# Bucketed attention with a gated MoE: key penalties on ScalarE, and a key of its own for each piece of the first batch

## The chip, the cores and the metric

The kernel runs on one core of a Trainium2 chip. The metric is the device time of one execution in microseconds, the median of several runs. The core has five engines that run on their own and wait for one another through semaphores: TensorE (PE in the profile, PEld its weight loads), VectorE (DVE), ScalarE (ACT), GpSimd (POOL), and SyncE (SP), which issues the DMAs.

## The reference

Attention over 4 batches, 8 heads, 768 positions and 64 dimensions, in which a query sees only the keys of its own hash bucket, and then a product of two linear layers, multiplied by a third:

```
q_bits = (q @ proj) > 0          # 6 bits; the same for k
mask   = bucket(q) == bucket(k)  # 64 buckets
scores = where(mask, (q @ k.T) / 8, -1e9)
attn   = softmax(scores); attn /= sum(attn) + 1e-9
x      = (attn @ v), heads side by side  # 3072 x 512
out    = ((x @ w_a) * (x @ w_b)) @ w_out # 512 -> 1536 -> 512
```

All inputs and the output are float32.

## The kernel before

**Units of work.** A batch has four head pairs and three chunks of 256 positions; a unit is one chunk for two head pairs (a `half`), and holds 8 tiles (`qtile`): one head, 128 queries, all 768 keys. So there are 24 units and 192 tiles. After the two units of a chunk, its rows of x are complete (`su_end`: divide, transpose, split into two fp16 parts `xT`), and one MoE block (`moe`) follows for the chunk, in 12 steps f of 128 hidden columns each: 24 matmuls for the two products, a multiplication, and 6 matmuls with w_out.

**Keys and queries.** `kprep` makes for a head pair the transposed keys (`trk`) in two parts, a rounded one and the remainder, then the hash bits, then for each of the 64 buckets the number of differing bits. The contraction of the score matmul has 128 rows: 64 for the head dimension, and 64 bucket rows. In the key's bucket rows stands a penalty: 0 where the bucket is the key's own and -2^60 where it isn't, made by VectorE (line 607) from the counts in PSUM. In the query's bucket rows stands a one-hot vector, made by ScalarE's Relu (line 708). So a score of another bucket gets -2^60 within the same matmul. `qprep` does a query half. In batch 0 both use one PSUM buffer (tag "o"), later a pair of them (tag "s") that the scores use too.

**A tile.** Scores into PSUM (4 matmuls, line 734); their negated maximum on VectorE (746); bias and exponential on ScalarE (753, 761); a cast to fp16 (line 775 on VectorE, or line 770 on ScalarE for tiles whose key is under `ACT_CASTS`, which is 0); the remainder on GpSimd (780); a transposing DMA (786); 18 matmuls with the two parts of v (795).

**Weights.** w_a and w_b come in 6 groups of 4 tiles of 128x512, w_out in 12 pieces (`wo_piece`). Each tile is loaded through one of 8 staging buffers (the first four pieces of w_out have their own place), converted by two ScalarE operations (347, 355) and one VectorE operation (362) that rebuild the number in another layout, and then split: w_a and w_b into two fp16 parts after a maximum over the group (392, 412, 417), w_out into two parts (428, 431). MoE step f needs the two groups of its third of the hidden columns, and its piece of w_out. All of that happens once, beside the first batch.

**The order.** Every operation is entered into a plan with its engine, an assumed duration, the buffers that it needs and a key, which is a priority and not a time: `Plan.issue` walks through an assumed time and, whenever an engine is free, gives it the operation with the lowest key among those that are ready and whose buffers can be had. What comes out is a fixed order for each engine (the DMAs in SP's too). Tile u of the unit that starts at `start` has the key `start + u`; a unit is 8 keys long. Preparations have keys some steps earlier (`K_LEAD`, `Q_LEAD`, `V_LEAD`), MoE blocks some later (`M_LAG`), the weight groups `W_FIRST + W_PACE * g`. `DVE_BESIDE` and `POOL_BESIDE` are what the plan adds where VectorE and GpSimd work on SBUF at the same time.

The key pairs of the first batch had the keys -7, -6.5, 1 and 3, its query halves -9, -1, 7, 15, 23 and 31, its v pairs -2, -1, 6 and 7; the weight groups 8, 10, 12, 14, 16 and 18, the pieces of w_out 20 (f 0 to 3), 24 and 28; the MoE blocks of the first two chunks 24 and 40, with 1.33 for each step.

Of the kernel before, what the change touches and what calls it, by code (L numbers as in the profile page):

```python
# [20 lines left out]
P = 128  # L21
# [10 lines left out]
NCH = S // CH  # L32
TPC = CH // P

NE, NA, NAT, NO = 3, 2, 2, 2
ACT_CASTS = 0
W_FIRST, W_PACE, WO_LAG = 8.0, 2.0, 8.0
M_LAG = 8.0  # L40
K_LEAD, Q_LEAD, V_LEAD = 7, 9, 2
S_LAG = -1.0
BIG = float(2.0**60)
ESC = float(2.0**14)
LN_ESC = float(14.0 * np.log(2.0))
# [3 lines left out]
def constants():  # L49

    c = np.zeros((P, P + 2), np.float32)
    c[:, :P] = np.eye(P)
    sets = (np.arange(NBUCK)[:, None] >> np.arange(NBITS)) & 1
    c[:, P] = 1 - np.tile(sets.sum(1), 2)
    c[:, P + 1] = -np.tile(sets.sum(1), 2)
    w = np.zeros((P, 2, P), np.float16)
    for j in range(2):
        for h in range(2):  # L60
            row = (2 * j + h) * NBITS
            col = NBUCK * (1 - h)
            w[row : row + NBITS, j, col : col + NBUCK] = 1 - 2 * sets.T
    return c, w
# [8 lines left out]
T_ISSUE = 1.4  # L73


DVE_BESIDE, POOL_BESIDE = 0.3, 0.15


class Buf:
# [140 lines left out]
def attention_moe(ctx: ExitStack, tc: tile.TileContext, q, k, v, proj, w_a, w_b, w_out, cst, cst_w, out):  # L220
# [19 lines left out]
    def flat2(ap):  # L240
        return ap.rearrange("p (a b) -> p a b", a=2)
# [181 lines left out]
    def wo_piece(f, key):  # L423

        y = buf("osb", [P, DM], F32, f"wo_y{f}", NO)
        after = [("words", f)] if f >= NF - NSTG else []
        to_f32(w_out[f * P : (f + 1) * P], f, f"wo{f}", key, lambda: y.t, [y], after)
        op("ACT", 0.6, lambda: nc.scalar.copy(out=wo[f].t[:, :DM], in_=y.t), key, r=[y], w=[(wo[f], 0)])
        op(
            "DVE", 0.7,  # L430
            lambda: nc.vector.tensor_tensor(
                out=wo[f].t[:, DM:], in0=y.t, in1=f32(wo[f].t[:, :DM]), op=ALU.subtract
            ),
            key, r=[y, (wo[f], 0)], w=[(wo[f], 1)], sbuf=True,
        )
# [75 lines left out]
    def kprep(b, hp, key, tag):  # L511

        n = f"{b}_{hp}"
        tr = [buf("trk", [P, 2, S], F32R, f"trk_{n}_{h}", NH) for h in range(2)]
        trk[b, hp] = tr
        raw = buf("raw", [P, NT, 2, D], F32, f"rk_{n}")
        for h in range(2):
            op(  # L520
                "SP", DMA_ISSUE,
                lambda h=h: nc.sync.dma_start(
                    out=raw.t[:, :, h, :], in_=k[b, 2 * hp + h].rearrange("(p t) d -> p t d", t=NT)
                ),
                key - 1, w=[(raw, h)], svc=1.1,
            )
        ps = psum(f"pk_{n}", tag)

        def tps():
            for t in range(NT):  # L530
                nc.tensor.transpose(  # L531
                    out=ps.t[:, t // 3, (t % 3) * P : (t % 3 + 1) * P],
                    in_=raw.t[:, t].rearrange("p h d -> p (h d)"), identity=ident,
                )

        op("PE", 0.7, tps, key, r=[(raw, 0), (raw, 1), "csb"], w=[ps], hold=tr)
        for h in range(2):
            op(
                "ACT", 0.81,
                lambda h=h: nc.scalar.activation(  # L540
                    flat2(tr[h].t[own[h], 0]), ps.t[own[h], :, :HALF], AF.Copy, scale=SCALE
                ),
                key, r=[ps], w=[(tr[h], "hi")],
            )
            op(
                "ACT", 0.81,
                lambda h=h: nc.scalar.activation(  # L547
                    flat2(tr[h].t[own[h], 1]), ps.t[own[h], :, :HALF], AF.Copy, scale=SCALE
                ),
                key, r=[ps], w=[(tr[h], "hi2")],  # L550
            )
            op(
                "DVE", 0.96,
                lambda h=h: nc.vector.scalar_tensor_tensor(  # L554
                    out=flat2(tr[h].t[oth[h], 1]), in0=ps.t[own[h], :, :HALF], scalar=SCALE,
                    in1=flat2(f32(tr[h].t[own[h], 0])), op0=ALU.mult, op1=ALU.subtract,
                ),
                key, r=[ps, (tr[h], "hi")], w=[(tr[h], "lo")],
            )
        exact = b == 0  # L560
        psb = psum(f"kb_{n}", tag)

        def rows():
            for j in range(2):
                cols = slice(j * HALF, (j + 1) * HALF)
                bit_rows(psb.t[:, j, :HALF], [(h, tr[h].t[:, 1, cols]) for h in range(2)], exact)

        op(
            "PE", 1.5 if exact else 0.75, rows, key,
            r=["pjw"] + [(tr[h], x) for h in range(2) for x in ("hi2", "lo")], w=[psb],  # L570
        )
        if exact:
            op(
                "DVE", 0.94,
                lambda: nc.vector.tensor_scalar(
                    out=flat2(bits_k[:NROW]), in0=halves(psb.t, NROW), scalar1=0.0, scalar2=None,
                    op0=ALU.is_gt,
                ),
                key, r=[psb], w=["bits_k"],
            )  # L580
        else:
            neg = buf("e", [P, S], F32, f"neg_{n}", NE)
            op(
                "ACT", 0.8, lambda: nc.scalar.mul(flat2(neg.t[:NROW]), psb.t[LOB:MB, :, :HALF], -1.0),
                key, r=[psb], w=[neg],
            )
            op(
                "DVE", 0.96,
                lambda: nc.vector.tensor_tensor(
                    out=flat2(bits_k[:NROW]), in0=halves(psb.t, NROW), in1=flat2(neg.t[:NROW]), op=ALU.is_gt  # L590
                ),
                key, r=[psb, neg], w=["bits_k"],
            )
        pso = psum(f"ko_{n}", tag)

        def diffs():
            for j in range(2):
                nc.tensor.matmul(
                    pso.t[:, j, :HALF], lhsT=wbit[:, 0, :], rhs=bits_k[:, j * HALF : (j + 1) * HALF],
                    start=True, stop=True,  # L600
                )

        op("PE", 0.35, diffs, key, r=["bits_k", "wbit"], w=[pso])
        for h in range(2):
            op(
                "DVE", 1.02,
                lambda h=h: nc.vector.tensor_scalar(
                    out=flat2(tr[h].t[oth[h], 0]), in0=pso.t[oth[h], :, :HALF], scalar1=neg_n[oth[h]],
                    scalar2=-BIG, op0=ALU.is_gt, op1=ALU.mult,
                ),  # L610
                key, r=[pso, "csb"], w=[(tr[h], "pen")],
            )

    def qprep(b, c, half, key, tag):
# [90 lines left out]
        for h in range(2):  # L705
            op(
                "ACT", 0.68,
                lambda h=h: nc.scalar.activation(  # L708
                    trq[h].t[oth[h], :, 0, :], flat2(pso.t[oth[h], 0]), AF.Relu, bias=one_n[oth[h]],
                    scale=-1.0,  # L710
                ),
                key, r=[pso, "csb"], w=[(trq[h], "hot")],
            )
# [231 lines left out]
    for b in range(NB):  # L945
        base = per * 6 * b
        for i, (c, half) in enumerate((c, half) for c in range(NCH) for half in range(2)):
            start = base + per * i
            tag = "o" if start < 2 * per else "s"
            if i < 2:  # L950
                for hp in (2 * half, 2 * half + 1):
                    kprep(b, hp, start - K_LEAD + (hp % 2) * (2 if b or half else 0.5), tag)
            qprep(b, c, half, start - Q_LEAD, tag)
            if i == 0:
                v_scale(b, start - 9 if b else -3)
            if i < 2:
                for hp in (2 * half, 2 * half + 1):
                    vprep(b, hp, start - V_LEAD + hp % 2)
            st = su_state(b, c, half)
            u = 0  # L960
            for j in range(2):
                for h in range(2):
                    for t in range(TPC):
                        qtile(b, c, half, j, h, t, st, start + u)
                        u += 1
            su_end(b, c, half, st, start + per - 1, "o" if start < 2 * per else "s")
            if b == 0 and i == 1:
                for g in range(NG):
                    w_group(g, W_FIRST + W_PACE * g)
                for f in range(NF):  # L970
                    wo_piece(f, W_FIRST + W_PACE * (f // 4 * 2 + 2) + WO_LAG)
            if half == 1:
                m = b * NCH + c
                moe(b, c, 2 * per * (m + 1) + M_LAG, 2 * per / NF, m == NB * NCH - 1)
    with tc.manual_schedule():
        plan.issue()

# [32 lines left out]
```

## Time and profile before

| | |
|---|---|
| median of 3 runs | 1033.65 us (1031.47 to 1034.38) |
| the profiled execution | 1032.79 us |
| its span, from the first to the last instruction | 1030.7 us |
| TensorE, weight loads | busy 941.3 us, 794.7 us |
| VectorE, ScalarE, GpSimd | busy 656.7, 597.7, 436.3 us |
| mean granted TensorE clock | 0.96 of full speed |

The profile is of one execution. "Busy" counts the time in which an engine works on an instruction, without register, branch and semaphore instructions. A row of a group of instructions gives line, engine, operation, output and input with their shapes, the count, then the summed busy time and the mean of one in ns, then the idle time of the engine just before them and what ended it.

### The profile page before, as it was taken

How to read it: one execution, taken by the hardware profiler on the slowest of the kernel's cores; microseconds unless marked ns; L12 is line 12 of the kernel's file. 1: busy time of each engine (PE TensorE's matmuls, PEld its weight loads, DVE VectorE, ACT ScalarE, POOL GpSimd, SP SyncE). 2: the span in 40 equal slices, each digit the busy share in tenths (PEclk: the TensorE clock that was granted, in tenths of full speed). 3: DMA queues.
4: the chain of work that ended last, by engine and by line, in shares of the span. 5: the costliest groups of instructions: out<-in, count | busy, mean ns of one | idle time of the engine just before them, and what ended most of it. 6: DMA issues, size and time to landing. Idle time of an engine off the chain costs nothing.

```text
span 1030.7 us, 22648 instructions
## 1 busy us (share of the span) xinstructions
PE 941.3 (91%) x9132; PEld 794.7 (77%) x9132; DVE 656.7 (64%) x984; ACT 597.7 (58%) x1251; POOL 436.3 (42%) x340
## 2 busy tenths in 40 slices
PE   3555568999999999999999999999999999999998
PEld 1434457888888888888788888888888888888886
DVE  3998999877767556557767556566776665544111
ACT  5787775656666655546666655556766655544221
POOL 0112344545544555544344445544435445455111
PEclk9757679999999999999999999999999999999999
DMA  8787766577565656676556666766556555565000
GB/s 286 239 205 210 160 136 109 90 149 171 104 132 113 110 105 128 113 149 124 123 93 130 103 99 123 149 128 129 116 124 113 103 113 93 98 122 96 16 22 21
DMA packets 370152, 127.44 MB, mean 124 GB/s; under 512 B 353920, under 2 KB 362368, under 8 KB 370048
## 3 DMA queue, kind: packets, MB, share of 16 engines
q1 hardware_dynamic: 370048, 126.00, 59.1%
q8 instruction: 72, 1.18, 0.5%
q14 instruction: 32, 0.26, 0.1%
HBM read 44.18 MB, written 6.29 MB: 49 GB/s over the span
## 4 chain that ended last, share of the span: by engine, by line
PE 77%; DVE 13%; ACT 7%; issue 2%; SPq 0%; DMA 0%; POOLq 0%; POOL 0%; DVEq 0%; ACTq 0%
PE ab L879 33%; PE o L921 18%; PE s L734 12%; PE av L795 8%; DVE trk L554 2%; ACT trk L540 2%; ACT trk L547 2%; PE qb L505 2%; DVE mx L746 1%; DVE wab L417 1%; PE kb L505 1%; DVE wab L362 1%; PE pq L638 1%; PE pk L531 1%; DVE a L775 1%
## 5 line engine op out<-in xcount | busy, mean ns | idle before, releaser
L780 POOL TENSOR_TENSOR a<-e,a 128x768 f16<-128x768 f32 x192 | 327.4, 1706 | 386.6 <-DVE a L775 316.4
L879 PE MATMUL ab<-xT,wab 128*128 128x256 f16 x3456 | 418.4, 274 | 1.7 <-DVE g L901 1.4
L879 PEld LDWEIGHTS <-wab 128*128 128x128 f16 x3456 | 325.0, 98 | 64.9 <-issue 28.6
L746 DVE TENSOR_REDUCE mx<-s 128x1 f32<-128x768 f32 x192 | 181.9, 951 | 103.5 <-PE s L734 102.0
L921 PE MATMUL o<-wo,g 128*128 128x512 f32 x864 | 233.4, 405 | 0.3 <-ACT g L908 0.2
L734 PE MATMUL s<-trk,trq 128*128 128x384 f32 x768 | 185.3, 368 | 30.6 <-ACT e L761 27.4
L911 POOL TENSOR_TENSOR g<-g,g 128x256 fp32r<-128x256 f32 x144 | 111.6, 775 | 201.7 <-ACT g L908 190.2
L761 ACT ACTIVATE e<-s,bias 128x768 f32<-128x768 f32 x192 | 172.9, 900 | 16.8 <-POOL a L780 6.4
L921 PEld LDWEIGHTS o<-wo,g 128*128 128x128 f32 x864 | 153.9, 189 | 27.9 <-ACT g L908 0.7
L734 PEld LDWEIGHTS s<-trk,trq 128*128 128x128 f32 x768 | 136.2, 200 | 38.9 <-ACT e L761 30.9
L901 DVE SCALAR_TENSOR_TENSOR g<-ab,absc,a 128x256 f32<-128x256 f32 x144 | 69.3, 481 | 138.9 <-ACT a L893 111.8
L753 ACT ACTIVATE bias<-mx,lnc 128x1 f32<-128x1 f32 x192 | 56.2, 293 | 171.4 <-DVE mx L746 170.7
L795 PEld LDWEIGHTS <-at 128*128 128x128 f16 x3456 | 124.0, 100 | 26.3 <-issue 21.2
L795 PE MATMUL av<-vh,at 128*128 128x64 f16 x2304 | 133.7, 196 | 1.4 <-DMA at<-a 1.2
L775 DVE CAST a<-e 128x768 f16<-128x768 f32 x192 | 117.9, 616 | 16.5 <-ACT e L761 9.8
L893 ACT ACTIVATE a<-ab,absc 128x256 f32<-128x256 f32 x144 | 68.2, 474 | 95.6 <-PE ab L879 94.0
L908 ACT CAST g<-g 128x256 fp32r<-128x256 f32 x144 | 58.0, 403 | 43.4 <-DVE g L901 41.4
L795 PE MATMUL av<-vl,at 128*128 128x64 f16 x1152 | 66.6, 195 | 1.7 <-DVE vl L491 1.7
L554 DVE SCALAR_TENSOR_TENSOR trk<-pk,trk 64x768 fp32r<-64x768 f32 x32 | 30.6, 955 | 29.8 <-ACT trk L547 20.7
L658 DVE TENSOR_TENSOR trq<-pq,trq 64x512 fp32r<-64x512 f32 x48 | 32.9, 686 | 19.1 <-ACT trq L653 16.9
L708 ACT ACTIVATE trq<-qo,csb 64x512 fp32r<-64x512 f32 x48 | 32.8, 683 | 15.2 <-PE qo L699 14.7
L648 ACT CAST trq<-pq 64x512 fp32r<-64x512 f32 x48 | 27.7, 578 | 21.2 <-PE pq L638 11.2
(77 smaller groups left out, 676.9 us busy)
## 6 DMA issues: line engine op xcount, KB each, us to landing
rq<-in_q_dram SPq DMA_DIRECT2D x96, 64.0 KB, 2.3
rk<-in_k_dram SPq DMA_DIRECT2D x32, 192.0 KB, 3.5
raw_w<-in_moe_w_a_dram SPq DMA_DIRECT2D x12, 512.0 KB, 6.2
raw_w<-in_moe_w_b_dram SPq DMA_DIRECT2D x12, 512.0 KB, 5.6
raw_wo<-in_moe_w_out_dram SPq DMA_DIRECT2D x12, 512.0 KB, 4.3
vm<-in_v_dram SPq DMA_DIRECT2D x16, 384.0 KB, 3.8
vr<-in_v_dram SPq DMA_DIRECT2D x16, 384.0 KB, 3.4
out_dram<-osb SPq DMA_DIRECT2D x24, 256.0 KB, 2.3
```

Source lines behind the costliest of these rows:

```text
L734: nc.tensor.matmul(ps.t[:, jj, :HALF], lhsT=trq.t[:, j, i, t * P : (t + 1) * P], rhs=tr.t[:, i, jj * HALF : (jj + 1) * HALF], start=i == 0 ...
L746: lambda: nc.vector.tensor_reduce(out=mx.t[:, u : u + 1], in_=halves(ps.t), axis=AX.XY, op=ALU.max, negate=True),
L761: lambda: nc.scalar.activation(flat2(e.t), halves(ps.t), AF.Exp, bias=bias.t[:, u : u + 1], scale=1.0, accum_out=sm.t[:, u : u + 1],),
L775: "DVE", 0.55, lambda: nc.vector.tensor_copy(out=a2.t[:, 0], in_=e.t), key,
L780: lambda: nc.gpsimd.tensor_tensor(out=a2.t[:, 1], in0=e.t, in1=a2.t[:, 0], op=ALU.subtract),
L795: nc.tensor.matmul(av.t[:, u, :], lhsT=at.t[:, a + kt, :], rhs=w.t[:, h, kt, :], start=i == 0, stop=i == 3 * NT - 1,)
L879: nc.tensor.matmul(pl.t[:, m, :CH], lhsT=wt(m, wi, cc, f), rhs=xi.t[:, cc, :], start=i == 0, stop=i == 3 * NC - 1,)
L893: lambda a=a, pl=pl, gr=gr: nc.scalar.activation(a.t, pl.t[:, 0, :CH], AF.Copy, scale=absc[:, b, gr : gr + 1]),
L901: lambda a=a, g32=g32, pl=pl, gr=gr: nc.vector.scalar_tensor_tensor(out=g32.t, in0=pl.t[:, 1, :CH], scalar=absc[:, b, gr + 1 : gr + 2], in ...
L908: op("ACT", 0.41, lambda g=g, g32=g32: nc.scalar.copy(out=g[0].t, in_=g32.t), kf - 8, r=[g32], w=[g[0], "order_g0"])
L911: lambda g=g, g32=g32: nc.gpsimd.tensor_tensor(out=g[1].t, in0=g32.t, in1=f32(g[0].t), op=ALU.subtract),
L921: nc.tensor.matmul(po.t[:, u, :], lhsT=g[gi].t[:, us], rhs=wo[f].t[:, wi * DM : (wi + 1) * DM], start=f == 0 and i == 0, stop=f == NF - 1 ...
```

## The change

- The penalties are made by ScalarE: Sign of (-count - n) with the bias n per row, which gives 0 for the own bucket and -1 for others. The factor 2^60 moves into the queries' one-hot rows: Relu with a scale of -2^60 and a bias multiplied by 2^60.
- In the first batch each key pair, query half, v pair, weight group, third of w_out and MoE block gets a key of its own.
- The casts of the first 16 tiles (keys under 16) go to ScalarE.
- In the later batches keys are prepared 10.5 steps ahead (7 before), queries 5 (9 before); MoE blocks lag by 7 (8 before).
- The plan assumes 0.5 and 0.25 us for VectorE and GpSimd beside one another (0.3 and 0.15 before).

```diff
-ACT_CASTS = 0
-W_FIRST, W_PACE, WO_LAG = 8.0, 2.0, 8.0
-M_LAG = 8.0
-K_LEAD, Q_LEAD, V_LEAD = 7, 9, 2
+ACT_CASTS = 16
+K_LEAD, Q_LEAD, V_LEAD = 10.5, 5, 2
+M_LAG = 7.0
+K0 = [-11.5, -8.5, -6.5, 6.5]
+V0 = [-2.0, -1.5, 7.0, 8.5]
+Q0 = [-5.5, 2.5, 11.0, 11.0, 29.5, 33.0]
+VS0 = -3.0
+WG0 = [11.0, 9.0, 11.5, 14.0, 19.5, 23.0]
 S_LAG = -1.0
+WO0 = [13.5, 17.0, 39.0]
+M0 = [19.0, 40.0]
+M0_PACE = [1.48, 1.33]
...
-    c[:, P] = 1 - np.tile(sets.sum(1), 2)
+    c[:, P] = BIG * (1 - np.tile(sets.sum(1), 2))
...
-DVE_BESIDE, POOL_BESIDE = 0.3, 0.15
+DVE_BESIDE, POOL_BESIDE = 0.5, 0.25
...
-                "DVE", 1.02,
-                lambda h=h: nc.vector.tensor_scalar(
-                    out=flat2(tr[h].t[oth[h], 0]), in0=pso.t[oth[h], :, :HALF], scalar1=neg_n[oth[h]],
-                    scalar2=-BIG, op0=ALU.is_gt, op1=ALU.mult,
+                "ACT", 0.81,
+                lambda h=h: nc.scalar.activation(
+                    flat2(tr[h].t[oth[h], 0]), pso.t[oth[h], :, :HALF], AF.Sign,
+                    bias=neg_n[oth[h]], scale=-1.0,
...
-                    scale=-1.0,
+                    scale=-BIG,
...
-                    kprep(b, hp, start - K_LEAD + (hp % 2) * (2 if b or half else 0.5), tag)
-            qprep(b, c, half, start - Q_LEAD, tag)
+                    kprep(b, hp, start - K_LEAD + 2 * (hp % 2) if b else K0[hp], tag)
+            qprep(b, c, half, start - Q_LEAD if b else Q0[i], tag)
...
-                v_scale(b, start - 9 if b else -3)
+                v_scale(b, start - 9 if b else VS0)
...
-                    vprep(b, hp, start - V_LEAD + hp % 2)
+                    vprep(b, hp, start - V_LEAD + hp % 2 if b else V0[hp])
...
-                    w_group(g, W_FIRST + W_PACE * g)
+                    w_group(g, WG0[g])
                 for f in range(NF):
-                    wo_piece(f, W_FIRST + W_PACE * (f // 4 * 2 + 2) + WO_LAG)
+                    wo_piece(f, WO0[f // 4])
...
-                moe(b, c, 2 * per * (m + 1) + M_LAG, 2 * per / NF, m == NB * NCH - 1)
+                first = m < len(M0)
+                moe(
+                    b, c, M0[m] if first else 2 * per * (m + 1) + M_LAG,
+                    M0_PACE[m] if first else 2 * per / NF, m == NB * NCH - 1,
+                )
```

## Rows read from the trace of the kernel before

**Rows 1.** The head of the page: span, then busy time and share of each engine.
```profile
span 1030.7 us, 22648 instructions
PE 941.3 (91%) x9132; PEld 794.7 (77%) x9132; DVE 656.7 (64%) x984; ACT 597.7 (58%) x1251; POOL 436.3 (42%) x340
```

**Rows 2.** Busy time by stage: stretch, its length, engines, clock, DMA share, GB/s.
```profile
0.00:153.00 153.00, 80.05 (x521) 59.22 (x522) 126.41 (x181) 111.74 (x202) 35.57 (x22) 0.74 0.77 206
153.00:190.00 37.00, 32.82 (x329) 27.09 (x327) 36.73 (x53) 23.39 (x49) 17.95 (x12) 0.95 0.56 101
190.00:940.00 750.00, 742.69 (x7584) 637.65 (x7582) 476.37 (x719) 441.71 (x954) 362.36 (x283) 1.00 0.62 119
940.00:1031.00 91.00, 85.76 (x707) 70.78 (x704) 17.21 (x33) 20.88 (x49) 20.41 (x24) 1.00 0.13 30
```

**Rows 3.** The same table for parts of the first 153 us.
```profile
30.00:153.00 123.00, 70.14 (x489) 54.02 (x490) 114.45 (x163) 93.46 (x173) 35.37 (x18) 0.68 0.75 183
20.00:90.00 70.00, 36.24 (x176) 25.47 (x177) 62.97 (x91) 58.03 (x103) 11.07 (x6) 0.72 0.87 251
...
20.00:153.00 133.00, 74.74 (x501) 56.15 (x502) 121.29 (x170) 102.26 (x188) 35.37 (x18) 0.70 0.77 200
```

**Rows 4.** Waits of 0 to 153 us: who for whom, total us, times, longest.
```profile
POOL a L780 <- DVE a L775: 105.5, 12, 38.5
```

**Rows 5.** Timeline of ScalarE at 152 us: start, length, instruction.
```profile
151.87 0.59 ACT L842 CAST xT<-px 128x512 f16<-128x512 f32 x1 [2.02 <-PE px L831]
```

**Rows 6.** Groups of VectorE, 0 to 153 us.
```profile
L362 DVE SCALAR_TENSOR_TENSOR wab<-raw_w 128x512 int32<-128x512 int32 x23 | 20.1, 883 | 2.2 <-ACT raw_w L355 1.9
L746 DVE TENSOR_REDUCE mx<-s 128x1 f32<-128x768 f32 x21 | 19.8, 948 | 1.2 <-PE s L734 1.0
L417 DVE SCALAR_TENSOR_TENSOR wab<-wab,wsc 128x512 f16<-128x512 f32 x20 | 18.9, 945 | 0.0
L775 DVE CAST a<-e 128x768 f16<-128x768 f32 x18 | 12.0, 665 | 0.1
L392 DVE TENSOR_REDUCE wmx<-wab 128x1 f32<-128x2048 f32 x5 | 11.4, 2275 | 0.1
L607 DVE TENSOR_SCALAR trk<-ko,csb 64x768 fp32r<-64x768 f32 x8 | 8.1, 1016 | 0.4 <-PE ko L598 0.2
```

**Rows 7.** Groups of ScalarE, 0 to 153 us.
```profile
L761 ACT ACTIVATE e<-s,bias 128x768 f32<-128x768 f32 x20 | 18.0, 900 | 3.7 <-POOL a L780 3.0
L355 ACT ACTIVATE raw_w<-raw_w 128x512 int32<-128x512 uint8 x24 | 15.9, 661 | 0.0
...
L412 ACT ACTIVATE wab<-wab,wsc 128x512 f16<-128x512 f32 x20 | 14.3, 716 | 4.9 <-DVE wab L417 4.7 <-DVE wsc L321 0.2
L347 ACT ACTIVATE raw_wo<-raw_wo 128x512 f32<-128x512 f32 x11 | 7.4, 670 | 1.4 <-DMA raw_wo<-in_moe_w_out_dram 1.4
...
L540 ACT ACTIVATE trk<-pk 64x768 fp32r<-64x768 f32 x8 | 6.4, 805 | 11.0 <-PE pk L531 6.6 <-DVE trk L554 4.4
...
L486 ACT ACTIVATE vh<-vr,vs 128x768 f16<-128x768 f32 x4 | 3.7, 921 | 0.4 <-DVE vs L321 0.4
```

**Rows 8.** Timeline of TensorE: first query half and key pair, first scores of both halves.
```profile
6.09 1.44 PE L638 MATMUL pq<-csb,rq 128*128 128x128 f32 x4 [6.09 <-DMA rq<-in_q_dram]
...
15.96 1.54 PE L531 MATMUL pk<-csb,rk 128*128 128x128 f32 x6 [1.47 <-ACT trq L708]
...
29.72 1.65 PE L734 MATMUL s<-trk,trq 128*128 128x384 f32 x4 [0.26 <-DVE trk L607]
...
88.03 2.88 PE L734 MATMUL s<-trk,trq 128*128 128x384 f32 x8 [1.92 <-DVE trk L607]
```

**Rows 9.** Groups of TensorE, 300 to 940 us.
```profile
L734 PE MATMUL s<-trk,trq 128*128 128x384 f32 x556 | 127.0, 352 | 0.8 <-ACT e L761 0.7
```

**Rows 10.** One line by itself, 0 to 190 us: shortest, median, longest in ns.
```profile
L417 DVE SCALAR_TENSOR_TENSOR wab<-wab,wsc x23: 729/737/2126, 47.0 to 182.2; 128x512 f16<-128x512 f32 x23
```

**Rows 11.** Groups of ScalarE over the whole span: the only table load.
```profile
L648 ACT ACT_TABLE_LOAD x1 | 1.3, 1283 | 0.7 <-PEq L989 0.7
```

## The prediction

> **What bounds the kernel now.** I read four views, in this order. The head of the page first: TensorE is busy 91% of 1030.7 us, VectorE 64%, ScalarE 58%, so in the mean TensorE is the bound [rows 1]. Then the table by stage, which shows that this mean mixes two regimes [rows 2]. From 190 to 940 us TensorE is busy 742.69 of 750 us at full clock, and nothing that relieves another engine can be worth more there than the 7.3 us that are left. From 0 to 153 us it is busy 80.05 us at a mean granted clock of 0.74: 73 us idle. Between lies a short ramp (37 us, 4.2 idle), and the last 91 us have 5.2 idle. The third view says who fills the first 153 us: VectorE, busy 114.45 of the 123 us between 30 and 153 (93%); ScalarE is at 76% there, and at 83% in its dense stretch from 20 to 90 us [rows 3]. The waits of this stretch agree: GpSimd stood 105.5 us for the fp16 cast on VectorE [rows 4]. The fourth view is the event that ends the regime. The chunk of x that the first MoE block needs is cast at 151.87 us [rows 5], and its matmuls start there. So the bound of the start is the work of VectorE, with ScalarE close behind, up to that event; the rest is TensorE's own work.
>
> What can't have been needed by then is in the same place: at 153 us VectorE has unpacked 23 of the 24 weight tiles and split 20 of them, and has reduced 21 score tiles, where the first chunk needs 16 [rows 6]. The weights went ahead of the attention.
>
> **The change, part by part.**
>
> *Penalties to ScalarE.* Each key pair has two, 1016 ns on VectorE, 8 in the first batch [rows 6]: 8 x 1.016 = 8.1 us off VectorE before the event. The trace has no Sign. The nearest row is ScalarE's copy of the same shape from PSUM, 64x768 to fp32r with a plain scale, 805 ns; the split of v, 768 columns with a scale read per partition as the bias is here, takes 921 [rows 7]. Nothing below the copy is to be had for the same columns, so 0.80 to 0.92 us; I take 0.81: 8 x 0.81 = 6.5 us onto ScalarE (at most 7.4). The 24 of the later batches move beside a full TensorE: ScalarE has 441.7 busy of 750 there [rows 2], 24 x 0.81 = 19 us take it from 59 to 61%. Cost nothing; without TensorE as cover it would be those 19 us.
>
> *One-hot rows scaled by 2^60.* Same instruction, another constant: nothing.
>
> *Casts to ScalarE.* The first 16 tiles' casts: 16 x 0.665 = 10.6 us off VectorE [rows 6]. ScalarE's row for it doesn't exist before; the ends are again the copy of 768 columns with a plain scale, 0.805, and the v split, which writes the same 128x768 fp16, 0.921 [rows 7]. The scale is plain here, so 0.82: 16 x 0.82 = 13.1 us (to 14.7). The cast now follows its exponential on the same engine instead of queueing behind weight work, which is the longest wait of [rows 4]; what is late next is ScalarE itself.
>
> *Order of the weights.* Groups 4 and 5 go from the keys 16 and 18 to 19.5 and 23, the wo pieces of f 8 to 11 from 28 to 39. Before, they already stood behind the first 16 tiles (keys 0 to 15) and were done first all the same, because the second half's scores waited for their key pair until 88.03 us [rows 8]; that pair's key goes from 1 to -6.5. By 153 us VectorE had spent on groups 4 and 5: 7 unpackings, 4 splits and one maximum, 7 x 0.883 + 4 x 0.945 + 2.275 = 12.2 us [rows 6]. ScalarE: 8 x 1.32 + 4 x 0.716 = 13.4 us, and the two conversions of 7 of the 11 wo pieces, 7 x 1.33 = 9.3 us [rows 7]. The order is by key only among what is ready, so a part is still done early, in the gap that the next paragraph shows. Between none and all of it I take two thirds, as all these keys move back and the gate of the second half's scores opens earlier: 8.1 us on VectorE, 15.1 on ScalarE. Of the tiles beyond 16 (5 reductions x 0.948, 4 exponentials x 0.900) half: 2.4 and 1.8 us [rows 6, 7].
>
> *Order of the preparation.* Three key pairs now stand ahead of the first query half. All use one PSUM buffer (tag "o"), one after the other: before, the query half took 6.09 to 15.96 us and the first pair 15.96 to its first scores at 29.72 [rows 8]. Three pairs of 14 us and the query's 10 put the first score tile at about 6 + 42 + 10 = 58 us. SP loads in the same order, with two raw buffers, and the v loads come behind them. That gap is filled by weight work (24 tiles, each with 1.8 us of VectorE, 0.883 + 0.945, and 2.0 of ScalarE, 2 x 0.661 + 0.716); what it costs if the cover fails is the second rival.
>
> *The sum.* VectorE up to the event: 126.4 - 8.1 - 10.6 - 8.1 - 2.4 = 97.2 us. ScalarE: 111.7 + 6.5 + 13.1 - 15.1 - 1.8 = 114.4 us [rows 2]. VectorE, with 11.9 us done by 30 us (126.4 - 114.45) and 93% from then on, would be there at 122 us, so ScalarE decides now. By 20 us it has done 9.5 (111.74 less the 102.26 of 20 to 153 [rows 3]); the other 104.9 at 93%, what the engine that binds reached, with its own 83% as the lower end, last 113 us: 133 us. The event comes 20 us earlier. Two score tiles fewer lie done then, 8 matmuls of 0.228 us (127.0 over 556) [rows 9] = 1.8 us that TensorE still has to do. Gain 18 us: 1032.79 - 18 = 1015 us. The profiled execution lies 0.9 us under the median of the three runs, 1033.65, so I leave it at 1015.
>
> *Later batches.* Key preparation 3.5 keys earlier, query preparation 4 later. A key is 4.6 us there (139 tiles in 640 us [rows 9]), so 5 keys of lead are 23 us for a chain of 10. Bounds: the 7.3 us idle of 190 to 940 all gone, or doubled; I take zero. MoE one key earlier leaves 4.6 us less behind the last attention tile: 0 to +4.6, I take zero. The new allowances for VectorE beside GpSimd only alter the order. What they deal with is real: a split takes 737 ns in the median and 2126 beside GpSimd [rows 10]. The mean of 945 over that median is 4.2 us on the 20 splits by 153 us; bounds 4.2 either way, on VectorE, which is not the bound of my sum.
>
> **Table loads.** The trace has one activation table load, 1283 ns at the start, and Exp, Prelu, Relu, Copy and Identity run behind it without another [rows 11]. The Trainium skill, ScalarE: Activation LUTs, section Table sets, says that functions come in named sets and that each switch of set costs about 2.7 us with its drain; its list for the set of exp gives only some of its functions, and Sign is not among those named. With Sign in the set my sum stands; without it, at the page's price, 4 pairs x 2 switches add an estimated 21 us to ScalarE. A rule of the same page, that cheap functions sit in every set, speaks for the first. The rival below goes by the row.
>
> **The rivals.**
> 1. *Larger gain.* All of the deferred weight work and all tiles beyond 16 stay behind the event: ScalarE has 111.7 + 19.6 - 22.7 - 3.6 = 105.0 us, 20 + 95.5/0.93 = 123 us, 30 us earlier, less 4 tiles or 3.6 us: 1006 us; with the key pairs ready sooner, down to 990. For it: the later keys. Against: idle engines take whatever is ready. The end of this road is 73 us.
> 2. *Slower: ScalarE becomes the bound behind a late first score.* Scores start near 58 us, and ScalarE stays at 83% with nothing deferred: 131.3 us of work, 20 + 121.8/0.83 = 167 us, 14 us later than now, with no tile fewer done: 1047 us. It decides from the point where the chunk is cast after 151 us. For it: 83% is what this engine reached [rows 3]; exponential and cast now cost it 0.90 + 0.82 = 1.7 us for each tile. Against: the bottleneck VectorE gives up 18.7 us, and the casts no longer queue.
> 3. *Gain given back in the ramp.* The chunk is ready early, but group 4 and 5 and the late wo pieces aren't: 12.2 us on VectorE and 8 wo pieces, each with an unpacking of 0.883 and a remainder of the same 512 columns, for which I take the same (14 us), fall into the 40 us after the event, where VectorE is 99% busy already (36.73 of 37) [rows 2, 6]. If half of those 26 us shows, 1015 + 13 = 1028 us.
> 4. *Sign is in another set.* 8 to 16 loads of 1.283 us on the ScalarE of the first batch, at 93%: 11 to 22 us, 1026 to 1037.
>
> **How the numbers follow.** Forecast (1007 to 1025) 0.50; rival 1 (990 to 1007) 0.24; rival 3 0.13; rival 2 0.10; rival 4 0.03. The range reaches into rival 1 to 991 and past rival 3 to 1036, and leaves out rival 2 and a tail below. About 0.3%, 3 us, is what a measurement can tell from no change. Faster than that: 0.50 + 0.24 + half of rival 3 and a third of rival 4 = 0.82; within: the middle of rival 3 and a share of rival 4, 0.07; slower: rival 2 and what is left, 0.11.
>
> **What would show it.** The cast of the first chunk near 133 us; TensorE over 90% busy within 10 us of it; ScalarE over 88% from 20 us to there and VectorE under it; Sign at 0.8 us and a single table load; first score near 58 us; 190 to 940 us unchanged. The prediction is wrong if the cast comes after 150 us, if TensorE idles more than 10 us in the 40 us behind it, or if the time moves with those marks in place.

## The result, and the profile after

The changed kernel takes 1020.29 us (median of 4 runs, 1019.93 to 1020.85) against 1033.59 for the kernel before: ratio 0.9875, 95% interval 0.9858 to 0.9892, 13.3 us less. The forecast was 1015 us, 18 less.

The head of the page, beside [rows 1]:

```profile
span 1018.4 us, 22624 instructions
PE 937.7 (92%) x9132; PEld 790.6 (78%) x9132; DVE 611.0 (60%) x936; ACT 634.8 (62%) x1299; POOL 433.0 (43%) x340
```

VectorE lost 45.7 us and ScalarE gained 37.1; TensorE is still busy for all but 81 us (89 before). Busy time by stage, beside [rows 2, 3]; the columns are those of [rows 2]:

```profile
0.00:143.00 143.00, 75.42 (x514) 53.77 (x514) 98.09 (x145) 116.01 (x203) 32.20 (x22) 0.75 0.75 199
143.00:190.00 47.00, 44.36 (x450) 37.67 (x451) 44.48 (x67) 36.86 (x77) 25.18 (x18) 0.96 0.76 163
190.00:930.00 740.00, 734.16 (x7475) 629.92 (x7474) 449.06 (x692) 460.79 (x972) 355.24 (x279) 1.00 0.62 119
...
20.00:143.00 123.00, 70.38 (x498) 51.28 (x498) 92.32 (x133) 107.13 (x191) 32.00 (x18) 0.71 0.73 187
...
930.00:1018.40 88.40, 83.73 (x697) 69.21 (x695) 19.39 (x34) 21.16 (x48) 20.37 (x23) 0.99 0.16 35
```

The two engines have changed places: from 20 us to the end of the first stage ScalarE is busy 107.13 of 123 us (87%), VectorE 75%. Two numbers carry the comparisons below. From 190 us on the granted clock is full, so TensorE's busy time from there to the end is the work that the start left undone: 734.16 + 83.73 = 817.9 us here, 742.69 + 85.76 = 828.5 before [rows 2]. The rest of the span behind 190 us is TensorE's idle time: 1018.4 - 190 - 817.9 = 10.5 us here, 12.2 before. So of the span's 12.3 us, 10.6 come from work done earlier and 1.7 from less idle time later.

Timeline of TensorE at the first scores and of ScalarE at the cast that completes the first chunk, beside [rows 5, 8]:

```profile
55.38 2.93 PE L744 MATMUL s<-trk,trq 128*128 128x384 f32 x8 [0.77 <-ACT trq L718]
...
142.72 0.59 ACT L852 CAST xT<-px 128x512 f16<-128x512 f32 x1 [0.20 <-PE px L841]
```

The first score comes at 55 us (58 forecast), the chunk at 142.7 (133 forecast, 151.87 before). The groups of ScalarE and then of VectorE from 0 to 143 us, beside [rows 7] and [rows 6]:

```profile
L357 ACT ACTIVATE raw_w<-raw_w 128x512 f32<-128x512 f32 x21 | 13.9, 664 | 0.1
...
L780 ACT CAST a<-e 128x768 f16<-128x768 f32 x16 | 13.2, 824 | 0.4 <-DMA at<-a 0.4
L422 ACT ACTIVATE wab<-wab,wsc 128x512 f16<-128x512 f32 x16 | 11.4, 711 | 0.1
L617 ACT ACTIVATE trk<-ko,csb 64x768 fp32r<-64x768 f32 x8 | 7.2, 896 | 5.7 <-PE ko L608 5.7
...
L357 ACT ACTIVATE raw_wo<-raw_wo 128x512 f32<-128x512 f32 x5 | 3.3, 660 | 0.0
...
L550 ACT ACT_TABLE_LOAD x1 | 1.3, 1283 | 0.7 <-PEq L1003 0.7
```

```profile
L756 DVE TENSOR_REDUCE mx<-s 128x1 f32<-128x768 f32 x21 | 20.0, 952 | 6.2 <-PE s L744 6.0
L427 DVE SCALAR_TENSOR_TENSOR wab<-wab,wsc 128x512 f16<-128x512 f32 x16 | 14.7, 921 | 5.6 <-ACT wab L422 5.5
L372 DVE SCALAR_TENSOR_TENSOR wab<-raw_w 128x512 int32<-128x512 int32 x19 | 13.0, 695 | 3.0 <-ACT raw_w L365 2.9
```

Sign takes 896 ns, the cast 824, and there is one table load. Of groups 4 and 5 nothing is split yet (16 splits are groups 0 to 3), and 5 pieces of w_out are begun instead of 11: the deferral took place. The score tiles are as many as before, 21 reductions.

### The profile page after: what moved, and what is told of

It reads as the page before. It is cut to its first block, busy times and chain, and to the rows that moved or that the text cites. A ratio compares the mean times of both kernels' runs of the same rounds, so it can differ in the third digit from the quotient of the medians.

```text
span 1018.4 us, 22624 instructions
## 1 busy us (share of the span) xinstructions
PE 937.7 (92%) x9132; PEld 790.6 (78%) x9132; DVE 611.0 (60%) x936; ACT 634.8 (62%) x1299; POOL 433.0 (43%) x340
## 4 chain that ended last, share of the span: by engine, by line
PE 76%; ACT 5%; DVE 3%; issue 1%; DMA 0%; POOL 0%; POOLq 0%; DVEq 0%; ACTq 0%
PE ab L889 34%; PE o L931 18%; PE s L744 11%; PE av L805 8%; DVE trk L564 1%; ACT trk L550 1%; ACT trk L557 1%; PE qb L515 1%; PE px L841 1%; PE pq L648 1%; ACT e L771 1%; PE kb L515 1%; ACT trk L617 1%; PE qo L709 0%; DMA at<-a 0%
## 5 line engine op out<-in xcount | busy, mean ns | idle before, releaser
L790 POOL TENSOR_TENSOR a<-e,a 128x768 f16<-128x768 f32 x192 | 323.4, 1684 | 374.0 <-DVE a L785 214.6
L805 PEld LDWEIGHTS <-at 128*128 128x128 f16 x3456 | 121.9, 99 | 33.2 <-issue 22.1
L785 DVE CAST a<-e 128x768 f16<-128x768 f32 x176 | 105.9, 602 | 40.9 <-ACT e L771 34.3
L718 ACT ACTIVATE trq<-qo,csb 64x512 fp32r<-64x512 f32 x48 | 32.8, 684 | 15.9 <-PE qo L709 15.4
L550 ACT ACTIVATE trk<-pk 64x768 fp32r<-64x768 f32 x32 | 25.7, 805 | 24.6 <-DVE trk L564 13.8
```

The source lines that it names most:

```text
L785: "DVE", 0.55, lambda: nc.vector.tensor_copy(out=a2.t[:, 0], in_=e.t), key,
L790: lambda: nc.gpsimd.tensor_tensor(out=a2.t[:, 1], in0=e.t, in1=a2.t[:, 0], op=ALU.subtract),
L805: nc.tensor.matmul(av.t[:, u, :], lhsT=at.t[:, a + kt, :], rhs=w.t[:, h, kt, :], start=i == 0, stop=i == 3 * NT - 1,)
```

## The experiments

Twelve kernels. "Keys" are the first batch's. "Left" is TensorE's busy time from 190 us to the end, "idle" the rest of the span behind 190 us, both of the one profiled execution; the median and the ratio to the kernel before (95% interval) are of all runs. Each kernel was timed beside fresh runs of the kernel before, whose median was 1033.1 us for Sign, Sign + casts, - Sign - casts and - casts, 1032.3 for Sign in batches 1 to 3, - Sign, - keys and - later leads, and 1032.4 for the last four; the ratios go by these.

| kernel | median us | ratio | chunk cast at | left | idle |
|---|---|---|---|---|---|
| before | 1033.6 | | 151.9 | 828.5 | 12.2 |
| the change | 1020.29 | 0.9875 [0.9858, 0.9892] | 142.7 | 817.9 | 10.5 |
| before + Sign | 1028.69 | 0.9960 [0.9947, 0.9973] | 155.1 | 827.4 | 9.1 |
| before + Sign in batches 1 to 3 | 1029.25 | 0.9968 [0.9956, 0.9979] | 151.2 | 828.1 | 9.8 |
| before + Sign + casts | 1029.52 | 0.9966 [0.9953, 0.9979] | 159.1 | 829.9 | 8.7 |
| change - Sign - casts | 1037.45 | 1.0037 [1.0023, 1.0052] | 151.4 | 827.5 | 19.3 |
| change - casts | 1030.26 | 0.9978 [0.9969, 0.9988] | 152.6 | 826.6 | 13.9 |
| change - Sign | 1034.41 | 1.0019 [1.0010, 1.0029] | 153.0 | 826.8 | 15.9 |
| change - keys | 1032.22 | 0.9995 [0.9985, 1.0004] | 158.2 | 832.0 | 8.5 |
| change - later leads | 1023.77 | 0.9910 [0.9895, 0.9925] | 145.2 | 820.5 | 12.4 |
| change, allowance 0.45 | 1028.03 | 0.9959 [0.9946, 0.9973] | 147.5 | 823.3 | 15.1 |
| change, old allowances | 1026.26 | 0.9936 [0.9922, 0.9951] | 144.4 | 821.0 | 14.5 |
| change, 8 casts | 1026.29 | 0.9937 [0.9922, 0.9951] | 149.6 | 823.3 | 11.7 |
| change, two PSUM tags | 1029.15 | 0.9960 [0.9947, 0.9974] | 147.8 | 825.1 | 13.0 |

**Sign alone, on the old keys.** The three hunks of the penalty and the one-hot rows, and nothing else:

```diff
-                "DVE", 1.02,
-                lambda h=h: nc.vector.tensor_scalar(
...
+                "ACT", 0.81,
+                lambda h=h: nc.scalar.activation(
+                    flat2(tr[h].t[oth[h], 0]), pso.t[oth[h], :, :HALF], AF.Sign,
...
-                    scale=-1.0,
+                    scale=-BIG,
```

> The kernel before with one part of the change: penalties by Sign on ScalarE and 2^60 in the one-hot rows; keys, casts and allowances as before. Load theory (the start lasts as long as the engine with the most work up to the first chunk of x): VectorE loses 8 x 1.016 us, at 93% the chunk comes 8.7 us earlier, 1025 us (1022 to 1028). Order theory (the start lasts as long as the attention's own chain, which the keys set; loads have slack): 1030 to 1035.

1028.69 us lies between the two, and neither is how it came about. The chunk came 3 us later, and the work left at 190 us is 1 us less; the gain is idle time behind 190 us, 12.2 to 9.1. That asked for the next one.

**Sign in the later batches alone.**

```diff
-                "DVE", 1.02,
+                "ACT" if b else "DVE", 0.81 if b else 1.02,
```

(with VectorE's form for b = 0, times -1.)

> The kernel before with Sign on ScalarE in the batches 1 to 3 alone; the first batch's 8 penalties stay on VectorE (times -1 instead of -2^60, the factor in the one-hot rows). Keys as before. The run with Sign everywhere gained 4.4 us, although its first chunk came 3 us later. Later-batch theory: those 24 penalties shorten the key chain in batches 1 to 3, TensorE's idle time of 190 to 930 us falls from 7.3 to about 4.5, and the whole is 1030 to 1031. First-batch theory: the gain comes from the start, this one stays at 1032 to 1034 with 7 us idle in 190 to 930.

1029.25: the later-batch theory, and a little more. The start is that of the kernel before (from 0 to 143 us TensorE is busy 74.57 us, 73.26 before; the chunk comes within 0.7 us of it). The waits of TensorE for the key remainder and its twin, between 190 and 930 us (who for whom, total us, times, longest), before and then in this kernel:

```profile
PE kb L505 <- DVE trk L554: 4.3, 5, 1.4
PE qb L505 <- DVE trq L658: 1.4, 2, 0.7
```

```profile
PE kb L505 <- DVE trk L554: 1.5, 2, 0.9
PE kb L505 <- ACT trk L547: 1.2, 1, 1.2
...
PE qb L505 <- DVE trq L661: 0.7, 1, 0.7
```

Here kb and qb are the hash bits of keys and queries. Before, it was VectorE that kept a key pair's bits waiting even where TensorE is 99% busy. With 24 penalties fewer TensorE waits there 1.5 us for VectorE and 1.2 for ScalarE, instead of 4.3 for VectorE.

**Sign and casts on the old keys.** As the first, with `ACT_CASTS = 16`.

> The kernel before with Sign and with the first 16 casts on ScalarE, all keys, leads and allowances as before. Load theory: VectorE loses 18.7 us, but ScalarE has 131 us of work up to the first chunk with nothing deferred, which at 93% ends at 151 us: no gain over the kernel before, 1028 to 1036. Order theory: 1028 to 1035 as well, the casts' shorter queue worth a few us at most. A third possibility, that engine placement is the whole effect: 1020.

1029.52: both theories had that range, so the time doesn't decide between them; the third possibility, 1020, is out. In the profile the chunk comes at 159.1 us, 7 later than before and 4 later than with Sign alone, so the casts bring the start nothing on the old keys.

**Keys, leads and allowances alone.** The changed kernel with `ACT_CASTS = 0` and VectorE's penalties.

> The changed kernel with the penalties back on VectorE and no casts on ScalarE: only keys, leads, lag and allowances are new. Load theory: VectorE has about 116 us up to the first chunk, which comes near 142 us, 1023 us (1019 to 1028). Order theory: the whole gain stands, 1018 to 1022. Placement is everything: 1031 to 1036.

1037.45, slower than before and above all three ranges. This order without the new division of work is no gain: the chunk stays at 151.4 us, and behind it TensorE idles 14.7 us between 190 and 930 us, twice what it did:

```profile
190.00:930.00 740.00, 725.33 (x7369) 622.26 (x7367) 461.21 (x701) 435.73 (x935) 344.73 (x273) 1.00 0.61 117
```

**The change without the casts.**

```diff
-ACT_CASTS = 16
+ACT_CASTS = 0
```

> The changed kernel with the first 16 casts back on VectorE. Load theory: ScalarE, the busiest of the changed start, loses 13.2 us and VectorE gains 10.6 us, so both stand near 105 us up to the first chunk; it comes near 135 us, 1012 us (1008 to 1017). Order theory: the casts queue behind weight work on VectorE again, and GpSimd with them; the chunk comes 5 to 10 us later, 1024 to 1030.

1030.26. The load theory, with its 1012, is out: with 13 us of casts taken from the busiest engine the chunk came 10 us later. The order theory's range ended at 1030. On these keys taking the casts off ScalarE costs 10 us, on the old ones nothing; but 6 to 9 us is what another order alone can cost (below), so the 10 are not shown to be the casts' own.

The load theory took ScalarE's other work as given, and it wasn't. The stretch up to the chunk, first in the changed kernel and then in this one, and under it this one's chunk and two groups of ScalarE from 0 to 153 us:

```profile
0.00:142.72 142.72, 75.42 (x514) 53.77 (x514) 97.81 (x144) 115.73 (x203) 31.92 (x22) 0.75 0.75 199
0.00:152.59 152.59, 78.86 (x513) 56.63 (x514) 117.55 (x181) 118.90 (x211) 36.32 (x22) 0.80 0.75 207
```

```profile
152.59 0.59 ACT L852 CAST xT<-px 128x512 f16<-128x512 f32 x1 [1.62 <-PE px L841]
L357 ACT ACTIVATE raw_w<-raw_w 128x512 f32<-128x512 f32 x24 | 15.9, 664 | 0.0
L357 ACT ACTIVATE raw_wo<-raw_wo 128x512 f32<-128x512 f32 x11 | 7.3, 666 | 0.0
```

ScalarE was busy 118.9 us up to the chunk, more than the 115.7 with the casts in it. All 24 tiles and 11 pieces of w_out were begun by then, against 21 and 5: weight work on ScalarE (conversions and splits) is 63.6 us instead of 48.0. The deferral went with the casts. Whether the weights went ahead because the attention was waiting, or the attention waited because they were ahead, these rows don't tell.

**The change without Sign.** The penalty hunks undone, casts and keys as changed.

> The changed kernel with the penalties back on VectorE; keys and casts as changed. Additive theory: Sign is worth 4 to 7 us, as between the runs without casts (1037.5 and 1030.3): 1024 to 1028. Joint theory (the keys fit only the full division of work): most of the gain is lost, 1029 to 1035. If casts and keys alone do it: 1020 to 1022.

1034.41, the joint theory: without Sign nothing is left of the gain. The chunk comes at 153.0 us, and TensorE idles 15.9 us behind 190.

**The change without its keys.**

```diff
-K0 = [-11.5, -8.5, -6.5, 6.5]
+K0 = [-7, -6.5, 1, 3]
...
-WG0 = [11.0, 9.0, 11.5, 14.0, 19.5, 23.0]
+WG0 = [8.0, 10.0, 12.0, 14.0, 16.0, 18.0]
```

(V0, Q0, WO0, M0 and its pace likewise.)

> The changed kernel with the first batch's keys of before (key pairs -7, -6.5, 1, 3 and so on); Sign, casts, later leads and allowances as changed. Additive theory: the keys cost 4 us by themselves, so this is faster than the change, 1014 to 1018. Joint theory: as Sign and casts on the old keys, 1028 to 1032, since the keys are what lets the casts on ScalarE pay.

1032.22: 0.2 us above the joint theory's range, and 14 above the additive one's. Timeline of this kernel, exponentials of ScalarE, and under it the maxima of the last two weight groups on VectorE:

```profile
61.38 0.89 ACT L771 ACTIVATE e<-s,bias 128x768 f32<-128x768 f32 x1
...
86.12 0.90 ACT L771 ACTIVATE e<-s,bias 128x768 f32<-128x768 f32 x1 [1.41 <-POOL a L790]
...
110.45 0.90 ACT L771 ACTIVATE e<-s,bias 128x768 f32<-128x768 f32 x1
```

```profile
75.32 2.29 DVE L402 TENSOR_REDUCE wmx<-wab 128x1 f32<-128x2048 f32 x1
89.15 1.75 DVE L402 TENSOR_REDUCE wmx<-wab 128x1 f32<-128x1536 f32 x1
```

The same two groups in the changed kernel:

```profile
145.29 2.27 DVE L402 TENSOR_REDUCE wmx<-wab 128x1 f32<-128x2048 f32 x1
172.21 1.74 DVE L402 TENSOR_REDUCE wmx<-wab 128x1 f32<-128x1536 f32 x1
```

On the old keys VectorE has the maxima of the last two groups, those of the last third of the hidden columns, done by 92 us, and one exponential starts between 62 and 110 us. On the new ones these groups come 70 and 83 us later, and ten exponentials start between 62 and 110 us. I take this for the lever of the change. The keys alone don't pull it: with the casts on VectorE the weights were early again and the chunk came at 152.6 us.

**The change with the old leads in the later batches** (`K_LEAD, Q_LEAD` 7 and 9, `M_LAG` 8).

> The changed kernel with K_LEAD 7, Q_LEAD 9 and M_LAG 8 of before in the later batches. My prediction put them at zero (bounds 7.3 us either way): 1018 to 1022. If the later leads cost (idle of 190 to 930 was 14.7 us with the new keys, leads and allowances alone): faster, 1015 to 1018; if they gain: 1022 to 1026.

1023.77, 3.5 us slower than the change. That is in the range of a gain from the leads. But its first chunk is 2.4 us later too, and the next two show that another order alone can cost as much and more, so I don't credit the leads with it.

**The same work in another order.** Two kernels change nothing but the plan's allowance for VectorE beside GpSimd; engines, keys and instructions stay.

```diff
-DVE_BESIDE, POOL_BESIDE = 0.5, 0.25
+DVE_BESIDE, POOL_BESIDE = 0.45, 0.25
```

> The changed kernel with one allowance of the plan, VectorE beside GpSimd, at 0.45 us instead of 0.5; all keys, leads and engines as changed. It alters no work, only the fixed order that the plan writes. Mechanism theory (keys and division of work make the gain, any good order has it): 1018 to 1023. Fit theory (part of the gain belongs to this one order, which the keys were fitted to): 1024 to 1030, with more of TensorE's work left at 190 us and the first chunk later than 142.7 us.

The second goes back to 0.3 and 0.15.

> The changed kernel with both allowances as before (0.3 and 0.15). The prediction had them at no more than 4.2 us either way. Mechanism theory: 1018 to 1024. Fit theory: 1024 to 1030, as far off as the smaller step of the allowance, since it is the order that is another and not the work.

1028.03 (0.45) and 1026.26: the fit theory, in both. Ratios of 0.9959 and 0.9936 against 0.9875 make 6 to 9 us, with the same work on the same engines. Stages of the kernel with 0.45:

```profile
0.00:143.00 143.00, 76.17 (x506) 54.72 (x506) 95.55 (x142) 114.67 (x199) 29.39 (x21) 0.83 0.75 204
...
143.00:190.00 47.00, 42.81 (x415) 36.87 (x416) 45.04 (x68) 36.96 (x77) 24.67 (x17) 0.91 0.66 140
190.00:930.00 740.00, 729.85 (x7425) 625.05 (x7424) 446.96 (x687) 460.78 (x966) 348.15 (x275) 1.00 0.62 118
```

and a wait in its ramp that is longer than in the change (1.3 us there):

```profile
155.44 2.72 PE L889 MATMUL ab<-xT,wab 128*128 128x256 f16 x12 [2.28 <-DVE g L911]
```

The loads are those of the change within 3 us; the loss is spread, 5.4 us in the work left and 4.6 in idle time behind 190 us.

**Half the casts.**

```diff
-ACT_CASTS = 16
+ACT_CASTS = 8
```

> The changed kernel with the casts of the first 8 tiles on ScalarE instead of 16; the 8 of the second half go back to VectorE (8 x 0.6 us), ScalarE loses 8 x 0.82 = 6.6 us. Load theory (ScalarE, 87% busy from 20 us to the first chunk, is the bound): the chunk comes up to 7 us earlier, 1014 to 1020. Latency theory (a cast behind its exponential saves the queue on VectorE, whatever the loads): later, 1023 to 1027, between the change and the run without casts (1030.3).

1026.29. The load theory (1014 to 1020) fails a second time: ScalarE has 6.6 us of casts less and the chunk comes 7 us later. Again the weights took the place: 58.9 us of weight work on ScalarE up to the chunk, 48.0 in the change. The latency theory's range holds the time, but so would another order.

**Preparations in two PSUM tags.**

```diff
-                    kprep(b, hp, start - K_LEAD + 2 * (hp % 2) if b else K0[hp], tag)
-            qprep(b, c, half, start - Q_LEAD if b else Q0[i], tag)
+                    kprep(b, hp, start - K_LEAD + 2 * (hp % 2) if b else K0[hp], "s" if b == 0 and hp == 1 else tag)
+            qprep(b, c, half, start - Q_LEAD if b else Q0[i], "s" if b == 0 and i == 0 else tag)
```

> The changed kernel with the second key pair and the first query half of the first batch in the PSUM buffers of the scores (tag s), which stand empty until the first score at 55.4 us, so that preparations no longer wait for one buffer. Chain theory (ScalarE's missing 13% is the chain of four preparations through one buffer): first score near 35 to 42 us, first chunk 3 to 8 us earlier, 1012 to 1018. Load theory: the first score comes earlier, but ScalarE's work up to the first chunk is the same and the weights take the place: 1018 to 1022. Fit theory: another order, 1022 to 1030.

1029.15, the fit theory's range. The timeline at its first scores, its longest wait of TensorE from 0 to 190 us, and the stretch from 20 us to its chunk:

```profile
38.10 2.77 PE L744 MATMUL s<-trk,trq 128*128 128x384 f32 x8 [2.06 <-ACT trq L718]
```

```profile
PE s L744 <- ACT e L771: 18.4, 10, 5.7
```

```profile
20.00:147.81 127.81, 73.75 (x486) 54.20 (x484) 98.80 (x140) 113.18 (x203) 30.04 (x18) 0.61 0.73 195
```

The first half of the chain theory holds (first score at 38 us, 17 earlier), the second does not: the chunk comes at 147.8 us, 5 later. The scores now wait 18.4 us for exponentials, 6.8 in the change. ScalarE did come to 89% (113.18 of 127.81), but with 56.4 us of weight work instead of 48.0. So neither the first score nor ScalarE's idle time sets the chunk by itself. No version beats the change.

## Why the prediction was right, and where it wasn't

**Right: the place.** All of the gain but 1.7 us came from the time up to 190 us, by the chunk that comes earlier and TensorE's earlier work: 10.6 us less left there. The first score (58 forecast, 55.4), the single table load, the first chunk as the event of the stage and the deferral of groups 4 and 5 came as written; the four rivals did not: ScalarE had begun 5 of the 8 late weight tiles and the score tiles were as many as before (in rival 1 none of either is early), ScalarE was at 87%, not 83%, TensorE idled 2.6 us in the 47 us behind the event, and Sign runs with the one table load. Of the signs, the chunk near 133 us and ScalarE over 88% did not come.

**Right: the terms of the sum on ScalarE.** 114.4 us were forecast up to the event, 116.0 are there by 143 us. The cast was taken at 0.82 (measured 0.824). Sign at 0.81 was 0.09 too low; with its bias read per partition it stands at 896 ns, close to the upper end, 0.92. The deferral was two thirds on ScalarE, as taken (15.5 of 22.7 us), and more on VectorE (9.6 of 12.2). The terms for fewer score tiles, 2.4 us on VectorE, 1.8 on ScalarE and 1.8 on TensorE, did not come: 21 reductions by the event, as before. And the 20 us by which the event was to come earlier were counted from 153, the end of the stretch; from the cast before, at 151.87, they are 19.

**Mis-sized: the rate.** The sum had ScalarE at 93% from 20 us on. It ran at 87%, and 8 of the 10 us by which the chunk came later than forecast went there: the 107.13 us at 93% end at 135 us, at 87% at 143. What ends most of its idle time is the preparation of keys and queries, each step on another engine; the longest of ScalarE's waits between 20 and 143 us, 9.0 of its 15.9 us of idle time:

```profile
ACT trk L617 <- PE ko L608: 3.4, 3, 1.7
ACT trk L550 <- DVE trk L564: 3.3, 2, 2.3
ACT trq L718 <- PE qo L709: 2.3, 4, 1.0
```

That 10.6 us less were left, for an event that comes only 9.2 earlier: TensorE was busy 119.8 us by 190 us (75.42 + 44.36), before 112.9 (80.05 + 32.82 [rows 2]), which is 6.9 more. The other 3.6 us is its busy time in all, 937.7 against 941.3 for the same 9132 matmuls; why it fell is not shown.

**Wrong: that the busiest engine sets the start.** The sum took the event as the work of the engine that binds, divided by a rate. Three kernels contradict that: without the casts' 13 us on ScalarE the chunk came 10 us later, without half of them 7 later, and with 8 us of penalties off VectorE (Sign on the old keys) 3 later; the two other orders of the same work moved it by 1.7 and 4.8 us, so the first is the clearest. Neither factor stands still. The rate was 93% (of VectorE) in one order and 83 to 89% (of ScalarE) in the change, its two other orders and the kernels without casts, with half of them and with two tags. And the work up to the event is no fixed sum from which a piece can be taken: what the casts left free went to weights, so that without them the deferral, a term taken at two thirds whatever the rest, was all but gone.

**Luck.** The event came 10 us later than forecast, and the gain was only 5 us short of it, since the sum had nothing for the ramp, for TensorE's shorter busy time and for the idle time behind 190 us, which all came out in its favour. And the measured time is that of one order: in two others of the same work, which the prediction took for equal within 4.2 us, it would have been 1026 or 1028 us, outside the 1007 to 1025 of the forecast, though inside the whole range of 991 to 1036.

**Wrong: the later batches at nothing.** The 24 penalties beside a full TensorE were costed at zero, since TensorE covers them. On three pairs of kernels that differ by Sign, idle time behind 190 us is lower with Sign each time: 12.2 to 9.8 (the later 24 alone, on the old keys), 19.3 to 13.9, 15.9 to 10.5. That is 2 to 5 us, against the zero taken; the last two pairs hold a change of order too. On the old keys it is nearly all that Sign is worth: by the ratios 3.3 us with the later 24 alone and 4.1 with all 32, and the intervals overlap. The allowances' bounds of 4.2 us were too narrow: a smaller step than theirs cost 8.

**How much belongs to what.** Sign, casts and keys don't add up. Taken out of the change, each costs 10 to 15 us, of which 6 to 9 may be the lost order. Put on the old kernel, Sign brings 4.4 us and Sign with casts 3.6 (on the medians), and the keys with leads and allowances lose 4.4. The two kernels of the same work in another order keep 4 and 7 of the 13 us (by the ratios), the one with the old leads 9. So I estimate that some 4 to 9 us belong to the change's mechanism (weights late, attention early, divided over both engines, and Sign behind 190 us) and the rest to the one order that these keys and allowances give; three neighbours are a small sample, and the split is not shown beyond them. Which decision in that order makes it better is open: the neighbours show where they lose, not why.

## What to carry to other kernels

In a kernel whose order comes from a list scheduler, a change of keys or engines is judged against its neighbours: make the same change with one assumed duration moved a little, several times, and don't credit the idea with what doesn't survive. A sum of an engine's work up to an event needs care where the scheduler has other work at hand: what a change frees may be filled with work that was meant for later. Work on an engine that is far from full is still on a chain: look at whom the instruction's reader waits for, even in a stage where the bound engine is 99% busy. And when a preparation can be put off until it is needed, it pays only if the engines that it leaves have the other work ready in that time.

## What the runs showed of the hardware

Sign with a bias per partition takes 896 ns on 64x768, the plain copy of the same shape 805: 91 ns more, which no run here divides between the function and the bias. The unpacking of a weight tile takes 695 ns in the mean here, against 883 before [rows 6], though its medians are alike, 681 and 687. Before, four of the 23 start while GpSimd's subtraction of line 780 runs and take 1.27 to 2.14 us, as here:

```profile
116.66 2.14 DVE L362 SCALAR_TENSOR_TENSOR wab<-raw_w 128x512 int32<-128x512 int32 x1
116.21 2.04 POOL L780 TENSOR_TENSOR a<-e,a 128x768 f16<-128x768 f32 x1 [3.48 <-ACT e L761]
```

Of the 19 in the changed kernel 11 start before 60 us, where GpSimd has not begun; the only one over 0.70 us (0.94) is the last, at 142.8 us, which starts while GpSimd runs (141.50 to 143.15).
